# Masked attention and soft mixture of experts in one kernel: maxima and sums of the first two pairs of heads without DMA

## The chip, the cores and the metric

The kernel runs on one core of a Trainium2 chip. The metric is device time in microseconds of one execution; the runs are given by their median.

## The reference

Eight batches of eight heads with 576 positions and 64 channels: attention with a causal mask and a bias that is a difference of running sums, then a soft mixture of eight experts over all 4608 rows.

```python
scores = scale * np.matmul(q, k.transpose(0, 1, 3, 2))
s_pos = np.maximum(s, 0.0)
cum = np.cumsum(s_pos, axis=-1)
bias = -(cum[:, :, :, None] - cum[:, :, None, :])
scores = np.where(causal, -1000000000.0, scores + np.minimum(bias, 0.0))
scores = scores - np.max(scores, axis=-1, keepdims=True)
attn = np.exp(scores)
attn = attn / (np.sum(attn, axis=-1, keepdims=True) + 1e-09)
attn_out = np.matmul(attn, v)
...
logits = x @ phi
slot_input = softmax(logits, 0).T @ x
slot_out[e] = np.maximum(slot_input[e] @ w1[e], 0.0) @ w2[e]
out = softmax(logits, 1) @ slot_out
```

All is fp32. The kernel multiplies with one pass in the rounded type fp32r where it carries a number as a high and a low part.

## The kernel before, in words

The heads go in 32 pairs; head 0 of a pair lies on partitions 0 to 63 and head 1 on 64 to 127, so two products run on the two row halves of TensorE. For pair p the steps are:

- `load` fetches q and k (576 KB) into one of two raw buffers. `cast` (L341, ACT) rounds q and k to fp32r, `low` (L347, DVE) keeps the rest. A raw buffer is free when both `low` of its pair are done.
- `cum` (L357, L360) brings the running sums of the pair's heads, as a high and a low row each, to the rows of the tile `g` on its right side (`KO`). The sums of all heads are scanned once at the start on DVE (L267 to L272, tile `cum`, heads on partitions 0 to 63), split into `cumhl`, and for pairs from 4 on fetched from a copy in DRAM (`cw`, L875).
- `mx` (L378), in four groups, gives the scores with the sums in PSUM: one product with w (q and k, rounded), one with `ones2` and `g`. `red` (L389, L392, DVE) takes from it the maximum for every query, with the mask. A group takes two PSUM banks; `mx`, the scores and the small products share six banks in turn.
- `f0` (L403, L404, POOL) splits the maxima, `f1` (L411) turns them on TensorE, `f2` (L417, ACT) copies them to `hl`, and `md` (L424, L427) moves `hl` by DMA into rows of `g`, left side. Every row of `g` is then an addend of the scores.
- `s` (L445), in four groups, gives the scores in four products: high by high, k low by q high, k high by q low, and `g` by `g`, which adds the sums and takes the maxima off. `ex` (L456, ACT) takes the exponential, `cut` (L463, POOL) masks the diagonal blocks, `zc` and `z` (L477, L484 to L490) add for the sums, `a` and `ax` (L533, L522) multiply with v into y and x, `sm` (L562) adds up the sums, `ev` and `evx` copy out.
- Every fourth pair, `rw`, `rd`, `nr`, `nat`, `lt`, `c0` to `t8` normalise, turn and reduce a batch for the mixture. After the last pair the experts' weights, which come in through `pre` and `get` (L860), go through two layers, and the output is written.

Nothing schedules this at run time. The list `ORDER` (from L24) names the steps in the order in which they are recorded; each engine's queue, and SP's queue of DMA issues, holds its steps in that order and runs them so. `busy.n` in the list (L937) is n fp32 products of the identity that nobody reads.

```python
        op(("load", p), load, [dep("low", g, 0), dep("low", g, 1), ("cum", 1) if p == 2 else None])
            op(("s", p, i), (sc, i), [("md", p), ("cum", p), ("low", p, 0), ("low", p, 1)])
```

## Time and profile before

| what | us |
|---|---|
| median of 3 runs | 415.88 (414.98 to 417.01) |
| the profiled execution | 415.59 |
| its span in the trace | 413.9 |
| TensorE busy (PE) | 395.3, 96% |
| DVE busy | 284.0, 69% |
| POOL busy | 274.8, 66% |
| ACT busy | 239.6, 58% |

The profiled execution is 415.59 us, of which the trace shows a span of 413.9. A row of the page's part 5 gives an engine's line, the tile written and the tile read, shapes, count, busy time, the mean of one, and how long the engine had stood idle before them. PE is TensorE, SPq the queue of DMA issues.

### The profile page before, as it was taken

The page shows a single profiled execution, that of the slowest core. Times are in us where ns is not written, and L with a number is a line of the kernel's source. Part 1 is how long each engine was busy: PE and PEld are TensorE (multiplying, and loading weights), DVE is VectorE, ACT ScalarE, POOL GpSimd, SP SyncE. Part 2 cuts the span into 40 slices and gives each one's busy share as a digit, 9 for nine tenths or more (in the row PEclk, how much of TensorE's full clock was granted, in tenths as well). Part 3 has the DMA queues.
Part 4 walks back from the last instruction along what each step waited for, and adds up shares of the span by engine and source line. Part 5 has one row for each costly group of instructions (what it writes and reads, how often), then busy time and mean ns, then how long its engine had stood idle before and what let it go on. Part 6 is the DMA issues. An engine that isn't in the chain of part 4 may idle for free.

```text
span 413.9 us, 14533 instructions
## 1 busy us (share of the span) xinstructions
PE 395.3 (96%) x5699; PEld 295.3 (71%) x5699; DVE 284.0 (69%) x952; ACT 239.6 (58%) x717; POOL 274.8 (66%) x376
## 2 busy tenths in 40 slices
PE   8999999999999999999999999999999999999950
PEld 8778777777787777777777787778777777435540
DVE  8956887877877787778767877787778547212460
ACT  3156766586768665866586768666865663220350
POOL 7069899888878888888788878887888740000000
PEclk9999999999999999999999999999999999999995
DMA  3424578526754475447644754463236789999998
GB/s 130 133 80 140 181 260 261 171 89 202 231 172 144 146 232 172 141 148 216 188 142 144 229 176 144 146 193 110 92 89 191 250 234 401 390 412 384 306 329 295
DMA packets 35252, 83.76 MB, mean 202 GB/s; under 512 B 4976, under 2 KB 14192, under 8 KB 35184
## 3 DMA queue, kind: packets, MB, share of 16 engines
q1 hardware_dynamic: 35168, 82.83, 60.6%
q8 instruction: 45, 0.74, 0.7%
q14 instruction: 23, 0.19, 0.1%
...
HBM read 72.43 MB, written 10.03 MB: 199 GB/s over the span
## 4 chain that ended last, share of the span: by engine, by line
PE 81%; DMA 4%; DVE 3%; ACT 2%; issue 2%; SPq 0%; DVEq 0%
PE s L445 25%; PE y L533 19%; PE mx L378 11%; PE sum L562 4%; PE m L1023 3%; PE m L995 3%; DMA g<-hl 3%; PE nat L601 3%; PE lt L666 2%; PE sl L786 2%; PE mt L411 1%; PE po L1061 1%; ACT arena L456 1%; PE x L522 1%; DVE arena L392 1%
## 5 line engine op out<-in xcount | busy, mean ns | idle before, releaser
L456 ACT ACTIVATE arena<-s 128x288 f32<-128x288 f32 (+4 forms) x384 | 114.9, 407 | 31.7 <-PE s L445 30.6
L445 PE MATMUL s<-w 64*128 64x288 f32 (+4 forms) x1152 | 109.2, 304 | 0.3 <-DVE nmin L743 0.2
L533 PE MATMUL y<-arena 128*64 128x512 f32 (+4 forms) x640 | 90.8, 427 | 0.0
L445 PEld LDWEIGHTS s<-w 64*128 64x128 f32 (+1 forms) x1152 | 81.9, 177 | 10.2 <-ACT arena L456 1.2
L463 POOL TENSOR_SCALAR_AFFINE_SELECT arena<-arena 128x256 f32<-128x256 f32 (+1 forms) x160 | 63.7, 411 | 23.6 <-ACT arena L456 22.0
L484 POOL TENSOR_TENSOR arena<-arena 128x896 f32<-128x896 f32 x31 | 69.3, 2237 | 8.7 <-PE mt L411 5.9
L533 PEld LDWEIGHTS y<-arena 128*64 128x64 f32 x640 | 42.5, 137 | 44.8 <-issue 34.1
L392 DVE CUSTOM_DVE_ANT_0 arena<-mx,arena 128x448 bf16<-128x448 f32 (+3 forms) x128 | 59.0, 461 | 17.6 <-PE mx L378 15.8
L378 PE MATMUL mx<-w 64*128 64x288 f32 (+4 forms) x384 | 56.6, 302 | 0.9 <-ACT w L341 0.9
L445 PE MATMUL s<-g 64*128 64x288 f32 (+4 forms) x384 | 56.5, 291 | 0.5 <-DMA g<-hl 0.5
L392 DVE CUSTOM_DVE_ANT_0 junk<-mx,arena 64x64 bf16<-64x64 f32 (+3 forms) x128 | 49.2, 385 | 10.4 <-PE mx L378 8.7
L378 PE MATMUL mx<-g,ones 64*128 64x288 f32 (+4 forms) x384 | 53.1, 300 | 0.0
L347 DVE TENSOR_TENSOR w<-arena,w 128x576 fp32r<-128x576 f32 x64 | 50.6, 810 | 0.2
L486 POOL TENSOR_TENSOR arena<-arena 128x640 f32<-128x640 f32 x31 | 48.3, 1557 | 2.4
L341 ACT CAST w<-arena 128x576 fp32r<-128x576 f32 x64 | 40.4, 677 | 13.7 <-DMA arena<-in_qk_dram 12.7
L545 ACT COPY arena<-y 128x512 f32<-128x512 f32 x32 | 18.8, 589 | 48.8 <-PE y L533 48.8
L389 DVE TENSOR_REDUCE mx<-mx 128x1 f32<-128x288 f32 x64 | 26.7, 447 | 27.5 <-PE mx L378 23.3
L378 PEld LDWEIGHTS mx<-w 64*128 64x128 f32 x384 | 38.5, 185 | 3.2 <-ACT w L341 1.0
L378 PEld LDWEIGHTS mx<-g,ones 64*128 64x128 f32 x384 | 38.2, 185 | 0.3
L445 PEld LDWEIGHTS s<-g 64*128 64x128 f32 (+1 forms) x384 | 35.1, 177 | 1.5 <-DMA g<-hl 1.0
L488 POOL TENSOR_TENSOR arena<-arena 128x384 f32<-128x384 f32 x31 | 31.8, 1026 | 2.4
L403 POOL TENSOR_SCALAR mh<-mx 128x10 fp32r<-128x10 f32 x32 | 20.1, 627 | 17.5 <-DVE mx L392 17.1
...
## 6 DMA issues: line engine op xcount, KB each, us to landing
...
```

The costliest lines, as they stand in the source:

```text
L341: nc.scalar.copy(w[:, o:o + S], st["raw", p][:, i, :])
L347: nc.vector.tensor_tensor(w[:, o + 2 * S:o + 3 * S], st["raw", p][:, i, :], w[:, o:o + S].bitcast(F32), op=ALU.subtract)
L378: nc.tensor.matmul(ps[a][:, d:d + hi - lo], l[r], t[r, k + lo:k + hi], start=t is w, stop=t is gt)
L389: nc.vector.tensor_reduce(m[:, a, c:c + 1], ps[:, d:d + w], axis=AX.X, op=ALU.max)
L392: nc.vector.tensor_tensor_reduce(out=junk()[r, 0:w], in0=ps[r, d:d + w], in1=mask[r, o:o + w], scale=1.0, scalar=m[:, a, 4:5] if i == 1 el ...
L445: nc.tensor.matmul(ps[a][0:n, d:d + hi - lo], t[r, ko + 128 * j:ko + 128 * j + n], t[r, qo + lo:qo + hi], start=x == 0, stop=x == 3)
L456: nc.scalar.activation(st["p", p][0:n, a, o + lo:o + hi], ps[0:n, d:d + hi - lo], AF.Exp, bias=0.0, scale=0.125)
L463: nc.gpsimd.affine_select(d, d, pattern=[[0, 2], [1, n]], compare_op=ALU.is_ge, fill=0.0, base=0, channel_multiplier=-1)
L484: eng.tensor_tensor(z[:, :, 128:576], pt[:, :, 128:576], pt[:, :, 576:1024], op=ALU.add)
L486: eng.tensor_tensor(z[:, :, 256:576], z[:, :, 256:576], pt[:, :, 1024:1344], op=ALU.add)
L488: eng.tensor_tensor(z[:, :, 384:576], z[:, :, 384:576], pt[:, :, 1344:1536], op=ALU.add)
L533: nc.tensor.matmul(y[r, lo - 64:512], vt[:, j, r], st["p", p][:, g, OFF[j] + lo - 128 * j:OFF[j] + 576 - 128 * j], start=(j == 0), stop=(j ...
```

## The change

For pairs 0 and 1 the sums and maxima no longer travel by DMA:

- The sums of the 64 heads are scanned on 128 partitions: head 0 of all pairs on partitions 0 to 31, head 1 on 64 to 95, in the regions of a `u` buffer. Two memsets on DVE clear the rows between, and s comes in two DMAs, one on ACT's queue.
- `mx` of pairs 0 and 1 multiplies `cum` itself, in fp32, by a column of the identity that is broadcast to 128; it needs no `cum` step. The scores still use `g`, whose sums come from `cumhl`; the split is now `ch.0` on ACT and `ch.1` on POOL.
- `low` of pairs 0 and 1 is on POOL instead of DVE.
- `f0` of pairs 0 and 1 is on DVE and writes the split maxima into a spread operand `turn`; `f1` is 20 fp32 products of 128x32 by 128 columns that put them on the rows of `g` where they belong, into two banks; `f2` and `md` copy the banks into `g` on ACT.
- The list of steps is another one up to about pair 8; the first filler is 12 products instead of 28, and three later fillers (9, 3 and 6) are gone.

The list's beginning, before and after (its other lines read alike):

```diff
-load.0 load.1 cast.0.1 cast.0.0 cast.1.1 low.0.1 cum.0 cast.1.0 low.0.0 cum.1 low.1.1 low.1.0 load.3 busy.28 mx.0.0
+load.0 load.1 cast.0.1 cast.0.0 ch.0 busy.12 mx.0.0 cast.1.1 mx.0.1 cast.1.0 red.0.0.0 red.0.0.1 mx.0.2 red.0.1.1
...
```

The code:

```diff
@@ -232,10 +232,14 @@
         return psm.tile([128, 512], F32, tag="bank", name=name)
 
 
-    s_sb = reg("x", 0)[0:NH, 0:S]
-    ones_s = reg("x", 0)[0:NH, S:2 * S]
-    cum = reg("x", 0)[0:NH, 2 * S:3 * S]
-    nc.sync.dma_start(out=s_sb, in_=s)
+    hb = ar["u", NP % NU]
+    s_sb = arena[:, hb:hb + S]
+    ones_s = arena[:, hb + S:hb + 2 * S]
+    cum = arena[:, hb + 2 * S:hb + 3 * S]
+    nc.vector.memset(s_sb[NP:64], 0.0)
+    nc.vector.memset(s_sb[64 + NP:128], 0.0)
+    nc.sync.dma_start(out=s_sb[0:NP], in_=s[0:NP])
+    nc.scalar.dma_start(out=s_sb[64:64 + NP], in_=s[NP:NH])
     nc.gpsimd.memset(ones_s, 1.0)
 
     QO, KO = PAD, PAD + S
@@ -267,20 +271,21 @@
     nc.vector.tensor_scalar(s_sb, s_sb, 0.0, 8.0, op0=ALU.max, op1=ALU.mult)
     nc.vector.tensor_tensor_scan(out=cum, data0=ones_s, data1=s_sb, initial=0.0,
                                  op0=ALU.mult, op1=ALU.add)
-    cumhl = reg("x", 0)[0:NH, 0:2 * S].rearrange("p (l x) -> p l x", l=2)
-    nc.vector.tensor_copy(cumhl[:, 0, :].bitcast(F32R), cum)
-    nc.vector.tensor_tensor(cumhl[:, 1, :].bitcast(F32R), cum, cumhl[:, 0, :], op=ALU.subtract)
-    cumd = pd.tile([NH, 2, S], F32, tag="cum", name="cumd", bufs=1)
+    cumhl = arena[:, hb:hb + 2 * S].rearrange("p (l x) -> p l x", l=2)
+    cumd = pd.tile([2, NP, 2, S], F32, tag="cum", name="cumd", bufs=1)
 
 
     for t in gs:
         nc.gpsimd.tensor_copy(t[:, 0:KO], ones2[:, 0:1].bitcast(F32).broadcast_to([128, KO]))
     SQ = S // 8
     onesl = one.tile([128, 4 * HP + 31], F32, name="onesl")
+    dn = one.tile([128, 2, 128], F32, name="dn")
+    x0 = ar["x", 0] + 2 * DM
+    turn = arena[:, x0:x0 + 128 * NCH].rearrange("p (c k j) -> p c k j", c=NCH, j=32)
+    nc.gpsimd.memset(turn, 0.0)
+    nc.gpsimd.memset(turn[:, :, :, 0], 1.0)
     nc.gpsimd.memset(onesl, 0.0)
     nc.gpsimd.memset(onesl[:, 4 * HP - 1:4 * HP], 1.0)
-
-    dn = one.tile([128, 2, 128], F32, name="dn")
     nc.gpsimd.memset(dn[64:128, 1, :], 0.0)
     nc.gpsimd.memset(reg("x", 0)[64:128, 0:DM], 0.0)
     for i in range(NPB):
@@ -314,6 +319,9 @@
 
     def every32(t, i):
         return t.bitcast(F32).rearrange("(a r) x -> a r x", r=32)[:, i, :]
+
+    op(("ch", 0), lambda: nc.scalar.copy(cumhl[:, 0, :].bitcast(F32R), cum))
+    op(("ch", 1), lambda: nc.gpsimd.tensor_tensor(cumhl[:, 1, :].bitcast(F32R), cum, cumhl[:, 0, :], op=ALU.subtract), [("ch", 0)])
 
     def scores(p):
 
@@ -344,7 +352,7 @@
             use("raw", p, NR)
             use("w", p, NW)
             o = (WQ, WK)[i]
-            nc.vector.tensor_tensor(w[:, o + 2 * S:o + 3 * S], st["raw", p][:, i, :],
+            (nc.gpsimd if p < 2 else nc.vector).tensor_tensor(w[:, o + 2 * S:o + 3 * S], st["raw", p][:, i, :],
                                     w[:, o:o + S].bitcast(F32), op=ALU.subtract)
         g = old(NW)
         war = [("s", g, i) for i in range(4)] if g is not None else []
@@ -352,16 +360,16 @@
             op(("cast", p, i), (cast, i), [("load", p)] + war)
             op(("low", p, i), (low, i), [("cast", p, i)])
 
-        def cum():
+        def cums():
             if p >= HP:
-                nc.sync.dma_start(out=every32(gt, 0)[:, KO:KO + S], in_=cumd[2 * p:2 * p + 2])
+                nc.sync.dma_start(out=every32(gt, 0)[:, KO:KO + S], in_=cumd[:, p])
                 return
             for a in range(2):
-                (nc.scalar if a and p == 0 else nc.sync).dma_start(out=every32(gt, 0)[2 * a:2 * a + 2, KO:KO + S],
-                                                                   in_=cumhl[2 * p + a:2 * p + a + 1, :, :])
+                nc.sync.dma_start(out=every32(gt, 0)[2 * a:2 * a + 2, KO:KO + S],
+                                  in_=cumhl[64 * a + p:64 * a + p + 1, :, :])
         g = old(NG)
         war = [("s", g, i) for i in range(4)] if g is not None else []
-        op(("cum", p), cum, war + [("cw",)] * (p >= HP))
+        op(("cum", p), cums, war + [("cw",) if p >= HP else ("ch", 1)])
 
 
         groups = [[(0, 4, 0, 288)], [(0, 4, 288, 576)], [(0, 3, 0, 448), (448, 0, 0, 64)],
@@ -373,10 +381,11 @@
             st["m", p, i] = ps
             for (d, c, lo, hi) in groups[i]:
                 q0 = WQ + sum(QC[c])
-                for l, t, k in ((w[:, q0 - 128:q0], w, WK), (ones2, gt, KO)):
+                for l, t, k in ((w[:, q0 - 128:q0], w, WK), (ones2, gt, KO) if p > 1 else (None, cum, 0)):
                     for a, r in enumerate(half):
-                        nc.tensor.matmul(ps[a][:, d:d + hi - lo], l[r], t[r, k + lo:k + hi],
-                                         start=t is w, stop=t is gt)
+                        x = ident[r, 64 * a + p:64 * a + p + 1].broadcast_to([64, 128]) if l is None else l[r]
+                        nc.tensor.matmul(ps[a][:, d:d + hi - lo], x, t[r, k + lo:k + hi],
+                                         start=t is w, stop=t is not w)
 
         def red(i, a):
             if i == 0 and a == 0:
@@ -393,12 +402,17 @@
                     out=junk()[r, 0:w], in0=ps[r, d:d + w], in1=mask[r, o:o + w], scale=1.0,
                     scalar=m[:, a, 4:5] if i == 1 else NEG, op0=ALU.add, op1=ALU.max, accum_out=m[r, a, c:c + 1])
         for i in range(4):
-            op(("mx", p, i), (mxp, i), [("cast", p, 0), ("cast", p, 1), ("cum", p), dep("f0", old(3))])
+            op(("mx", p, i), (mxp, i), [("cast", p, 0), ("cast", p, 1), ("cum", p) if p > 1 else None, dep("f0", old(3))])
             for a in range(2):
                 op(("red", p, i, a), (red, i, a), [("mx", p, i), ("red", p, 0, a) if i else None])
 
         def f0():
             use("mx", p, 3)
+            if p < 2:
+                mh = [turn.rearrange("p c (a l) j -> p a l c j", a=2)[:, :, l, :, 1] for l in range(2)]
+                nc.vector.tensor_scalar(mh[0].bitcast(F32R), m, 1.0, None, op0=ALU.mult)
+                nc.vector.tensor_tensor(mh[1].bitcast(F32R), m, mh[0], op=ALU.subtract)
+                return
             mh = p2.tile([128, 2, 2, NCH], F32R, tag="mh", name=f"mh{p}")
             nc.gpsimd.tensor_scalar(mh[:, :, 0, :], m, 1.0, None, op0=ALU.mult)
             nc.gpsimd.tensor_tensor(mh[:, :, 1, :], m, mh[:, :, 0, :].bitcast(F32), op=ALU.subtract)
@@ -406,6 +420,13 @@
         op(("f0", p), f0, [("red", p, i, a) for i in range(4) for a in range(2)] + [dep("f1", old(2))])
 
         def f1():
+            if p < 2:
+                st["mt", p] = [bank(f"mt{i}") for i in range(2)]
+                for c in range(NCH):
+                    for k in range(4):
+                        nc.tensor.matmul(st["mt", p][c // 4][32 * k:32 * k + 32, 128 * (c % 4):128 * (c % 4) + 128],
+                                         turn[:, c, k, :], ident, start=True, stop=True)
+                return
             mh = st.pop(("mh", p))
             ps = bank("mt")
             nc.tensor.transpose(ps[0:4 * NCH, 0:128], mh.rearrange("p a l c -> p (a l c)").bitcast(F32), ident)
@@ -413,19 +434,19 @@
         op(("f1", p), f1, [("f0", p), dep("md", old(2))])
 
         def f2():
+            if p < 2:
+                nc.scalar.copy(gt[:, 0:512], st["mt", p][0])
+                return
             hl = p2.tile([4 * NCH, 128], F32R, tag="hl", name=f"hl{p}", bufs=1)
             nc.scalar.copy(hl, st.pop(("mt", p))[0:4 * NCH, 0:128])
             st["hl", p] = hl
         op(("f2", p), f2, [("f1", p)])
 
         def md():
-            hl = st.pop(("hl", p))
-            if p:
-                nc.sync.dma_start(out=every32(gt, 1)[:, 0:KO].rearrange("l (c q) -> l c q", c=NCH), in_=hl.bitcast(F32))
+            if p < 2:
+                nc.scalar.copy(gt[:, 512:KO], st["mt", p][1][:, 0:KO - 512])
                 return
-            for a in range(2):
-                (nc.scalar if a and p == 0 else nc.sync).dma_start(out=every32(gt, 1)[2 * a:2 * a + 2, 0:KO].rearrange("l (c q) -> l c q", c=NCH),
-                                  in_=hl[2 * NCH * a:2 * NCH * (a + 1)].bitcast(F32))
+            nc.sync.dma_start(out=every32(gt, 1)[:, 0:KO].rearrange("l (c q) -> l c q", c=NCH), in_=st.pop(("hl", p)).bitcast(F32))
         op(("md", p), md, [("f2", p)])
 
 
@@ -872,7 +893,10 @@
     op(("sit", 0), sit0, [prev, ("t8", B - 1)])
     op(("sit", 1), sit1, [("sit", 0)])
     op(("cst",), (fetch, g4, cst[:, 0:128]), [("load", 3)])
-    op(("cw",), lambda: nc.sync.dma_start(out=cumd, in_=cumhl), [("cum", 1)])
+    def copy_cum():
+        for a in range(2):
+            nc.sync.dma_start(out=cumd[a], in_=cumhl[64 * a:64 * a + NP])
+    op(("cw",), copy_cum, [("cum", 1)])
     op(("phi",), load_phi, [("load", 2)])
     ops["lt", 0][1].append(("phi",))
 
@@ -1158,7 +1182,7 @@
     HP = H // 2
 
     phi = moe_phi.reshape(HP, 128, -1).transpose(1, 0, 2)
-    arrays = dict(qk=qk, v=vn, s=s.reshape(B * H, S), phi=phi, w1=w1, w2=w2, cst=constants())
+    arrays = dict(qk=qk, v=vn, s=s.reshape(B * H // 2, 2, S).transpose(1, 0, 2).reshape(B * H, S), phi=phi, w1=w1, w2=w2, cst=constants())
     return {n: np.ascontiguousarray(a) for n, a in arrays.items()}
```

What the change makes of two queues, as the built programs list them. First TensorE, from the last maxima of pair 1 that come ahead of the first scores (`s_0`); `mx_1` are maxima of pair 1, `w_101` and `w_104` its rounded q and k, `mt` the banks of the turn. Before:

```order
L378 MATMUL mx_1_0_296<-w_101 128x448
L378 MATMUL mx_1_1_297<-w_101 128x448
L378 MATMUL mx_1_0_296<-g_98,ones_109 128x448
L378 MATMUL mx_1_1_297<-g_98,ones_109 128x448
L378 MATMUL mx_1_0_296<-w_101 128x64
L378 MATMUL mx_1_1_297<-w_101 128x64
L378 MATMUL mx_1_0_296<-g_98,ones_109 128x64
L378 MATMUL mx_1_1_297<-g_98,ones_109 128x64
L937 MATMUL busy<-ident 128x128 x6
L445 MATMUL s_0_0_323<-w_100 128x288
```

Now:

```order
L387 MATMUL mx_1_0_217<-arena,ident 128x64
L387 MATMUL mx_1_1_218<-arena,ident 128x64
L427 MATMUL mt_236<-ident,arena 32x128 x16
L427 MATMUL mt_237<-ident,arena 32x128 x4
L387 MATMUL mx_1_0_269<-w_104 128x288
L387 MATMUL mx_1_1_270<-w_104 128x288
L387 MATMUL mx_1_0_269<-arena,ident 128x288
L387 MATMUL mx_1_1_270<-arena,ident 128x288
L466 MATMUL s_0_0_277<-w_103 128x288
```

The filler ahead of the first scores is gone, the 20 products of the turn stand two groups of products before them, and the last group of pair 1's maxima (320 and 192 columns) has moved behind the first scores.

Then POOL, from its last memsets to the first masks (`L463`, now `L484`); `mh` are the split maxima. Before:

```order
L285 MEMSET arena 64x512
L287 MEMSET arena 64x2x64 x2
L288 MEMSET acc 128x512
L403 TENSOR_SCALAR mh_257<-mx_115 128x2x5
L404 TENSOR_TENSOR mh_257<-mx_115,mh_257 128x2x5
L403 TENSOR_SCALAR mh_354<-mx_117 128x2x5
L404 TENSOR_TENSOR mh_354<-mx_117,mh_354 128x2x5
L463 AFFINE_SELECT arena<-arena 128x2x128 x3
```

Now:

```order
L290 MEMSET arena 64x512
L292 MEMSET arena 64x2x64 x2
L293 MEMSET acc 128x512
L324 TENSOR_TENSOR arena<-arena 128x576
L355 TENSOR_TENSOR w_103<-arena,w_103 128x576 x2
L355 TENSOR_TENSOR w_104<-arena,w_104 128x576 x2
L484 AFFINE_SELECT arena<-arena 128x2x128 x3
```

Four tiny instructions on the maxima have left POOL's queue, and five subtractions of 576 columns have come in ahead of the first mask.

## Rows read from the trace of the kernel before

**Rows 1.** The page: busy time of the engines, and the chain's shares by line.

```profile
PE 395.3 (96%) x5699; PEld 295.3 (71%) x5699; DVE 284.0 (69%) x952; ACT 239.6 (58%) x717; POOL 274.8 (66%) x376
...
PE s L445 25%; PE y L533 19%; PE mx L378 11%; PE sum L562 4%; PE m L1023 3%; PE m L995 3%; DMA g<-hl 3%; PE nat L601 3%; PE lt L666 2%; PE sl L786 2%; PE mt L411 1%; PE po L1061 1%; ACT arena L456 1%; PE x L522 1%; DVE arena L392 1%
```

**Rows 2.** TensorE's waits, whole span: us in total, times, longest us.

```profile
PE busy L937 <- POOL ident masks.py:199: 1.4, 1, 1.4
PE mx L378 <- ACT w L341: 0.9, 1, 0.9
```

**Rows 3.** The chain that ended last, 0 to 60 us: start us, us, what.

```profile
18.67 1.08 PE mx L378 x11
19.76 1.53 PE busy L937 x12
21.29 3.41 PE s L445 x48
...
25.33 0.21 PE mt L411
25.54 1.01 PE y L533 x4
...
29.64 2.81 PE s L445 x40
```

**Rows 4.** Stretch 350 to 380: busy of five engines, granted clock, DMA share, GB/s.

```profile
350.00:380.00 30.00, 29.80 (x342) 14.72 (x340) 7.78 (x22) 5.93 (x14) 0.45 (x1) 1.00 1.02 403
```

**Rows 5.** Timeline of the start, four engines: start us, us, instruction, count.

```profile
1.07 1.15 DVE L251 MEMSET g<- 128x576 f32 x2
...
4.50 1.67 DVE L268 TENSOR_TENSOR_SCAN arena<-arena 64x576 f32<-64x576 f32 x1
5.38 1.25 ACT L341 CAST w<-arena 128x576 fp32r<-128x576 f32 x2 [3.31 <-DMA arena<-in_qk_dram]
...
8.31 0.53 POOL L288 MEMSET acc<- 128x512 f32 x1
...
10.71 0.34 SPq L331 DMA_DIRECT2D arena<-in_qk_dram  x1
...
11.25 0.82 DVE L389 TENSOR_REDUCE mx<-mx 128x1 f32<-128x288 f32 x2 [0.56 <-PE mx L378]
...
15.17 0.62 DVE L392 CUSTOM_DVE_ANT_0 arena<-mx,arena 128x448 bf16<-128x448 f32 x1
...
16.09 0.82 DVE L389 TENSOR_REDUCE mx<-mx 128x1 f32<-128x288 f32 x2
...
17.22 0.67 ACT L341 CAST w<-arena 128x576 fp32r<-128x576 f32 x1 [7.32 <-DMA arena<-in_qk_dram]
...
22.50 2.81 ACT L456 ACTIVATE arena<-s 128x288 f32<-128x288 f32 x10 [3.88 <-PE s L445]
```

**Rows 6.** One line of POOL: shortest, median and longest ns, first and last start.

```profile
L277 POOL CAST g<-ones x3: 717/944/1771, 3.4 to 4.9; 128x640 fp32r<-128x640 f32 x3
```

**Rows 7.** The chain near 346 us: products of 128 columns, 32 rows of output each.

```profile
346.31 0.22 PE lt L666 x8
```

**Rows 8.** Line L937 in two stretches of the start: ns, first and last start.

```profile
L937 PE MATMUL busy<-ident x7: 421/421/421, 5.2 to 6.5; 128*128 128x128 f32 x7
L937 PE MATMUL busy<-ident x11: 274/275/275, 7.3 to 8.4; 128*128 128x128 f32 x11
```

**Rows 9.** Groups by form: count, busy us, mean ns, idle before.

```profile
L486 POOL TENSOR_TENSOR arena<-arena 128x640 f32<-128x640 f32 x31 | 48.3, 1557 | 2.4
L488 POOL TENSOR_TENSOR arena<-arena 128x384 f32<-128x384 f32 x31 | 31.8, 1026 | 2.4
L545 ACT COPY arena<-y 128x512 f32<-128x512 f32 x32 | 18.8, 589 | 48.8 <-PE y L533 48.8
```

**Rows 10.** Two stretches in which TensorE did nothing; the granted clock is third from the end.

```profile
18.00:18.60 0.60, 0.00 (x0) 0.00 (x0) 0.60 (x5) 0.60 (x2) 0.00 (x0) 1.00 0.00 0
404.00:406.00 2.00, 0.00 (x0) 0.00 (x0) 0.00 (x0) 0.00 (x0) 0.00 (x0) 0.50 1.01 345
```

More of the change, by code (lines that the diff above doesn't have):

```diff
@@ new lines @@
+low.29.0 f0.28 t4.5 s.27.2 ex.27.0.0 low.29.1 ex.27.0.1 s.27.1 load.31 ex.27.2.0 cut.27.0 mx.29.0 ex.27.2.1 sm.26
+ex.27.1.0 red.29.0.0 cut.27.2 red.29.0.1 ex.27.1.1 f1.28 t5.5 f2.28 cut.27.1 zc.27 s.27.3 md.28 t6.5 z.27.0 mx.29.3
+ex.27.3.0 cum.30 mx.29.2 ex.27.3.1 red.29.3.0 cast.30.1 mx.29.1 red.29.3.1 cast.30.0 a.26.0 cut.27.3 red.29.2.0 z.27.1
+a.26.1 red.29.2.1 a.26.2 a.26.3 z.27.2 red.29.1.0 a.26.4 ax.27 ev.26 load_v.28 red.29.1.1 s.28.0 low.30.0 evx.27
+z.27.3 s.28.2 low.30.1 ex.28.0.0 f0.29 ex.28.0.1 s.28.1 ex.28.2.0 get.0 cut.28.0 mx.30.0 ex.28.2.1 sm.27 ex.28.1.0
@@ L164 @@
+c0.7 t2.7 t3.7 busy.1 m.0 nat.31 t8.6 nat.28 m.1 nat.29 natd.31 natd.28 m.2 natd.29 nat.30 m.3 t4.7 nat0.7 m.4 natd.30
+c1.7 get.21 natd0.7 t5.7 m.5 get.22 t6.7 busy.2 m.6 t7.7 m.7 s0.7 s1.7 ct t8.7 get.26 get.19 get.17 get.10 sit.0
+get.24 get.25 get.23 sit.1 s2.7 s2p.7
 """
```

266 lines of the change are left out of this document (129 added, 137 removed).

## The prediction

> **What bounds the kernel now.** I read the page first: TensorE is busy for 395.3 of 413.9 us [rows 1]. The list of TensorE's waits then says how little of the rest is idling: the longest entries are 1.4 us for the identity at the start and 0.9 us for a cast [rows 2]. So the time is TensorE's queue, and an edit pays only by taking work off that queue or by filling it earlier. The chain of the first 60 us shows where it is filled with nothing: behind the first maxima stand filler products (L937), the first scores (L445) begin at 21.29 us, the second pair's at 29.64 [rows 3]. After 21.29 I see no wait of TensorE in that chain. What lies ahead of 21.29 is a latency chain over DVE, DMA and ACT, and the change works on that chain. From the maxima of pair 8 on, TensorE's order is the same in both programs, and the other engines' from about pair 9, so a lead that is there at pair 8 should reach the end.
>
> The tail must move too. From 350 to 380 us the DMA engines are at 1.02 of their share while TensorE works 29.80 of 30 us [rows 4]; those weight loads go into buffers that the last pairs free, so they are released earlier by the same amount.
>
> **The chain to the first scores, step by step.** Times are from the span's start.
>
> 1. *Sums.* The scan ends at 6.2 (4.50 + 1.67) [rows 5]. Two memsets of 576 columns now come ahead of it on DVE; two such took 1.15 [rows 5]. That gives cum at 7.3. The scan can also meet one of three like casts on POOL, of which the quickest took 717 ns and the slowest 1771 [rows 6]; against this stands that DVE waited a little for s there, which the memsets use up. I let the two cancel and keep 0.7, a whole cast, for the range. The Trainium skill (SBUF — State Buffer, "SBUF: two separate sides") says that a GpSimd instruction and a DVE one with two SBUF inputs shut each other out for their whole length; the 1771 agrees, and by that rule the sum would have cum at up to 8.0.
>
> 2. *First product.* It needs the casts of q and k (5.38 + 1.25 = 6.6) and now cum itself instead of two DMA landings. The fp32 products with cum are new; their nearest row is L533, fp32 on two column halves at once, 1.01 us for 512 columns [rows 3]. So 288 columns cost 0.57 and the first reduction can start at 7.9, where it started at 11.25. If the two row halves did not overlap, each price would double; I take the row's and keep the double for the range.
>
> 3. *Maxima of pair 0.* DVE ran them without a gap from 11.25 to 16.09, so 4.84 us [rows 5]. TensorE's share for a pair is about 0.7 for the half with w (L378 has 11% of the span for 32 pairs, 1.4 with both halves [rows 1]) plus 3.2 for 1600 columns with cum, 3.9 in all, less than DVE's 4.84; the third group, 0.25 + 1.01, comes some 0.3 after DVE is ready for it. End at 13.05. The split into high and low moves from POOL to DVE, two tiny instructions: 0.4, between nothing and the 0.8 of two reductions. 13.45.
>
> 4. *Turn.* Twenty fp32 products of 128x32 with 128 columns, 40 passes. The row of that shape is L666, 8 in 0.22 us [rows 7]: 1.1 us. One by one they would take 4.4, at the later pace of the filler (11 starts from 7.3 to 8.4, 0.11 each [rows 8]). L666 has the same four column groups, so I take 1.1: 14.55. Two ACT copies follow; the first (0.59 by L545 [rows 9]) can start when 16 of the 20 are done, the second has a quarter of its columns, 0.3. The row is in place at about 15.2. The DMA to the left side, behind which filler stood in the queue, is gone.
>
> 5. *Bank.* The first scores need PSUM banks that DVE frees only after four reductions of pair 1: 0.82 for the two short ones and 0.92 for each pair of 448 and 64 columns (15.17 to 16.09) [rows 5], 2.6 in all, from 13.45 to 16.05. This is later than 15.2, so it decides: **first scores at 16.05, 5.2 us earlier than 21.29.**
>
> 6. *POOL* now subtracts for cum and for both operands of pairs 0 and 1, five instructions of 576 columns. Between 1026 ns (384) and 1557 (640) [rows 9] that is 1.42, with gaps 1.5. Its memsets ended at 8.84 (8.31 + 0.53) [rows 5]; they start about 1.1 later behind DVE's memsets and get 0.8 more for the spread operand (640 columns, by the 0.53 of 512, and a short one), so 10.8; then 12.3 for cum, 15.3 for both operands of pair 0, 18.3 for pair 1. The scores use pair 0's low parts in their second and third product, so 15.3 is hidden by 16.05 with 0.7 to spare. DVE's 3 us for them leave its queue.
>
> **What is given back.** At 21.29 the old queue had done all maxima of pairs 0 and 1 and the first group of pair 2. At 16.05 the new one still owes the last group of pair 1 (512 columns: 0.25 + 1.0 = 1.25) and the first of pair 2 (0.4 of the 1.08 us in [rows 3]); and pair 1's turn costs 1.1 where L411 took 0.21: 0.9 more. That is 2.55. Filler is not counted: it fills waits.
>
> **New waits** between first and second scores: pair 1's maxima end behind its last fp32 group, about 0.3 us after TensorE is ready to turn them. The load of pair 2 has to wait for POOL's subtracts of pair 0 (two raw buffers), 15.3 instead of 10.71, and behind it in SP's queue stand v of pair 0, the load of pair 3 and cum of pair 2. Load 2 was issued at 10.71 and its cast ran at 17.22 with another load in flight; the first load, alone at the start, was cast at 5.38 [rows 5]. So load 2 lands some 4 to 5 us after 15.3, at 19 to 20. ACT comes to its cast at about 18.8 (16.05, 1.0 for 480 of the 1600 columns of the scores' 3.41, and 1.7 for six exponentials at 2.81 for ten [rows 3, 5]), and ACT's queue is in order: behind the cast stand exponentials that free banks and the copies of pair 1's turn. I put nothing for this in the sum and 1 us in a rival.
>
> **Sum.** 5.24 - 2.55 - 0.3 = 2.4 us. The profiled execution took 415.59 us (span 413.9), 0.29 under the median of 415.88. So 413.2 against the profiled one, and **413.5 against the median, 0.6% less**. About 0.5% (2.1 us) is what a measurement of this kernel can tell from no change.
>
> **The rivals.**
>
> *POOL and the loads keep back half.* At 1.9 each (the casts went up to 1771 [rows 6]), POOL's five end at 20.3 instead of 18.3: pair 0's low parts come at 16.5, the scores 0.5 late, and with loads 2 and 3 going out later ACT waits about 1 us for a cast. Gain 2.4 - 0.5 - 1 = 0.9: 415.0. For it: the whole chain of loads now hangs on POOL. Against it: DVE's reductions read PSUM and only a mask from SBUF, and the mean of L486 beside them is 1557 for the larger shape. 0.15.
>
> *The clock (slower).* The first filler products took 421 ns each, 275 from 7.3 us on [rows 8]: TensorE began at 1.2 GHz and rose to 2.4 while it worked without a pause. The granted clock reads 1.00 in the pause at 18.0 and 0.50 from 404 us on, after TensorE's last work [rows 10]. The change cuts the filler at the start from 28 to 12 products, 24 passes, which at the slow pace (7 starts from 5.2 to 6.5 [rows 8]) last to about 6.5; the queue then pauses for cum, near where the clock rose. If it stays at 1.2 GHz, the 7.6 us that TensorE does before the first scores (3.9 + 0.7 + 1.25 + 1.1 + 0.7) take 15.2: first scores near 22 with the same 2.55 owed, so 3.3 us *slower*: 419.2. It decides from where the low clock lasts to about 14.6 us: lost is half of the time after 7.3, less the 1.2 by which DVE is the slower in step 3. The Trainium skill (TensorE: Matmul & The Clock Gate, Part 1) says that the low clock is the default and activity releases it; the 421 and 275 agree. Against the rival: the queue is filled for most of 7.3 to 16. 0.12 for slower; 0.05 for a rise between, which eats the gain (415.9).
>
> *The end does not move.* If the saturated DMA of the tail held the end by itself, 2.4 us at the front would give nothing: 415.9. Against it: TensorE has no wait for a weight among its longest [rows 2], and the loads hang on buffers it frees. 0.04.
>
> **How the numbers follow.** The forecast has 0.64 and its own range from 411.7 to 414.4: the upper gain of 4.2 has the first scores at 15.2 (step 5's bank free in time) and only 1.9 owed (the last group of pair 1 at 0.6, as a group with `ones2`); the lower, 1.5, has an ACT wait of 0.9. I put 0.52 of the 0.64 past 2.1 us and 0.12 below. Faster 0.52; same 0.12 + 0.15 + 0.05 + 0.04 = 0.36; slower 0.12. The range of 8 in 10 goes from 411.2 to 416.0: it takes in the cases without gain and leaves out the low clock and a little below. Cum products at the double price (6.4 + 0.7 for pair 0, 2.3 over DVE's 4.84) and cum at 8.0 lie inside it too.
>
> **What would show it.** First product with cum near 7.4 and first reduction near 7.9; 40 passes of the turn in about 1.1 us; first scores at 16.0, the second pair's near 24.3 with 2.5 us of maxima and y still owed; POOL's last subtract near 18.3. Wrong would be: first maxima at twice their price past 9 us; an ACT wait of over 1 us for a load; scores before 15 or after 17.5; or pair 8 reached less than 1 us earlier although pair 1 was 2.4 earlier.

## The result

The changed kernel took 419.55 us (median of 5 runs, 418.92 to 420.93), the kernel before beside it 416.43 (414.98 to 417.16): ratio 1.0093, 95% interval 1.0069 to 1.0118. It is **slower by 3.1 us**; 413.5 had been predicted, with 416.0 as the upper end. The profiled execution after took 418.92 us (span 417.2).

TensorE's list of waits (us in total, times, longest us) names the places:

```profile
PE lt L687 <- DVE mx L401: 1.7, 1, 1.7
PE nat L622 <- DVE mx L401: 1.0, 1, 1.0
PE mt L427 <- DVE arena L414: 0.9, 1, 0.9
PE s L466 <- DVE mx L401: 0.5, 1, 0.5
```

Beside these there is again the identity's 1.4. Before, the longest after it was 0.9 for a cast [rows 2]; behind each of these four stands DVE. DVE's busy time doesn't show it: 285.3 us now, 284.0 then [rows 1].

**The start** came nearly as forecast. Its timeline (start us, us, engine, line, operation, count; in brackets the idle time before, and what ended it):

```profile
7.89 0.82 DVE L398 TENSOR_REDUCE mx<-mx 128x1 f32<-128x288 f32 x2 [0.84 <-PE mx L387]
12.13 5.51 POOL L355 TENSOR_TENSOR w<-arena,w 128x576 fp32r<-128x576 f32 x4
13.60 1.32 DVE L414 TENSOR_TENSOR arena<-mx,arena 128x10 fp32r<-128x10 f32 x1
14.97 1.29 PE L427 MATMUL mt<-ident,arena 128*32 128x128 f32 x38 [0.88 <-DVE arena L414]
16.70 0.78 PE L466 MATMUL s<-w 64*128 64x288 f32 x6
19.71 1.29 ACT L349 CAST w<-arena 128x576 fp32r<-128x576 f32 x2
```

The first scores start at 16.70, 4.6 us earlier than 21.29 [rows 3]. One row is odd: L414, DVE's subtraction of ten columns that makes the low half of the split, takes 1.32 us beside POOL's subtractions L355. Pair 1's, with POOL idle, takes 0.18.

**Then the lead goes in three steps.** The stretches, from the timelines of POOL, DVE and TensorE:

```profile
51.81 2.08 POOL L505 TENSOR_TENSOR arena<-arena 128x896 f32<-128x896 f32 x1
52.06 2.45 DVE L355 TENSOR_TENSOR w<-arena,w 128x576 fp32r<-128x576 f32 x1
57.97 0.85 PE L466 MATMUL s<-w 64*128 64x448 f32 x5 [0.50 <-DVE mx L401]
...
80.61 2.12 POOL L505 TENSOR_TENSOR arena<-arena 128x896 f32<-128x896 f32 x1
82.12 1.58 DVE L614 TENSOR_TENSOR arena<-arena 128x576 f32<-128x576 f32 x1 [1.36 <-DMA arena<-rs]
84.44 0.43 PE L687 MATMUL lt<-arena 128*32 128x128 f32 x8 [1.67 <-DVE mx L401]
...
278.12 2.12 POOL L505 TENSOR_TENSOR arena<-arena 128x896 f32<-128x896 f32 x1
278.26 2.60 DVE L614 TENSOR_TENSOR arena<-arena 128x576 f32<-128x576 f32 x1
281.60 0.66 PE L622 MATMUL nat<-ident,arena 128*128 128x128 f32 x4 [1.05 <-DVE mx L401]
```

Each time a DVE instruction with both operands in SBUF (`low`, L355; `nr`, L614) runs beside POOL's sums `z` (L505), and takes 1.6 to 2.6 us where 0.75 is usual. Below, such an overlap is called a **meeting**, and the instruction that it stretches is **shut out**. Behind it in DVE's queue stand the reductions of the maxima, and TensorE waits for the PSUM banks that they free. Two stretches (busy of five engines, granted clock, DMA share, GB/s) show that TensorE stands still for half of a microsecond at the first loss, and that behind the second it works at 0.50, its lower level of 1.2 GHz (the granted clock reads 0.76 from 85 to 86 and 0.53 from 88 to 89):

```profile
57.00:58.00 1.00, 0.50 (x9) 0.25 (x6) 0.94 (x5) 0.71 (x3) 0.09 (x1) 1.00 0.33 133
...
86.00:88.00 2.00, 2.00 (x21) 1.72 (x13) 1.94 (x9) 0.91 (x2) 0.28 (x2) 0.50 1.05 391
```

The kernel before has the same pair of instructions at the second place, and there it costs DVE nothing:

```profile
80.97 0.75 DVE L593 TENSOR_TENSOR arena<-arena 128x576 f32<-128x576 f32 x1
81.00 2.70 POOL L484 TENSOR_TENSOR arena<-arena 128x896 f32<-128x896 f32 x1
...
90.61 0.28 PE L411 MATMUL mt<-ident,mh 128*20 128x128 f32 x1
...
379.94 0.70 PE L1035 MATMUL sel<-pre 128*128 128x256 f32 x2 [0.18 <-DVE pre L1030]
```

DVE was first by 0.03 us; it is POOL's row that is longer, 2.70 for 2.12. The last two rows are marks of TensorE's progress, the turn of pair 8 and the selection near the end. In the kernel after they are:

```profile
93.05 0.28 PE L432 MATMUL mt<-ident,mh 128*20 128x128 f32 x1
...
382.98 0.70 PE L1059 MATMUL sel<-pre 128*128 128x256 f32 x2 [0.17 <-DVE pre L1054]
```

So TensorE is 2.4 us late at pair 8 and 3.0 at the end. The expectations below call this a **lag**: TensorE's matmuls are counted by columns through all its rows, and the lag at a moment of the kernel before is how much later (+) or earlier (-) the other kernel has as many still to issue. Up to pair 8, where the orders differ, the lag depends on how columns are counted, by about half a microsecond; from 91 us on it doesn't. The times are medians, the lags are from the profiled executions; e1 to e12 are the experiments that follow:

| kernel | us (ratio to before, interval) | 47 | 59 | 79 | 91 | 259 | 399 |
|---|---|---|---|---|---|---|---|
| after | 419.55 (1.0093, 1.0069 to 1.0118) | -1.1 | +0.6 | -0.6 | +2.4 | +1.9 | +3.0 |
| e1 | 414.18 (0.9961, 0.9938 to 0.9984) | -1.1 | -1.1 | -0.8 | -0.8 | -1.9 | -1.9 |
| e2 | 420.33 (1.0122, 1.0092 to 1.0152) | +1.5 | +3.4 | +2.2 | +5.4 | +4.4 | +4.4 |
| e3 | 416.15 (1.0013, 0.9987 to 1.0038) | -1.6 | +0.1 | -1.1 | +0.9 | -0.3 | -0.3 |
| e4 | 418.18 (one run) | -1.2 | +0.5 | -0.7 | +1.3 | +1.3 | +2.4 |
| e5 | 418.60 (1.0065, 1.0041 to 1.0088) | -1.1 | +0.6 | -0.6 | +2.7 | +1.8 | +2.8 |
| e6 | 416.27 (1.0006, 0.9988 to 1.0025) | -1.1 | -1.0 | -2.3 | -0.3 | -0.7 | +0.3 |
| e9 | 417.44 (1.0043, 1.0017 to 1.0070) | +0.2 | +1.9 | +0.7 | +2.9 | +2.3 | +3.4 |
| e8 | 413.54 (0.9938, 0.9917 to 0.9959) | -2.0 | -2.0 | -2.0 | -2.0 | -3.0 | -3.1 |
| e10 | 415.59 (0.9987, 0.9967 to 1.0007) | -1.1 | +0.7 | -0.6 | -0.3 | 0.0 | 0.0 |
| e12 | 417.03 (1.0029, 1.0002 to 1.0056) | -1.1 | +0.7 | -0.6 | +0.9 | +1.0 | +1.0 |
| e11 | 412.92 (0.9938, 0.9915 to 0.9960) | -1.3 | -1.2 | -2.4 | -2.0 | -3.0 | -3.0 |

The lag of one profiled execution and the medians can differ by a microsecond. e9, whose edit lies at 80 us, has 1.3 more already at 47, because TensorE's clock fell at its start: the turn takes 2.36 us there for the 1.29 above, and the first scores start at 18.21 instead of 16.70 (e9, a row and a stretch):

```profile
14.97 2.36 PE L427 MATMUL mt<-ident,arena 128*32 128x128 f32 x38 [0.89 <-DVE arena L414]
...
15.00:17.00 2.00, 2.00 (x38) 1.73 (x38) 1.91 (x7) 0.00 (x0) 2.00 (x2) 0.50 0.53 124
```

Between 155 and 203 us the profiled execution of the kernel before loses some 1.0 that e8 and e11 don't lose; their leads grow by that.

### The profile page after: what moved, and what is told of

The parts are those of the page before. It is cut to its first block, busy times and chain, and to the rows that moved or that the text cites. A ratio compares the mean times of both kernels' runs of the same rounds, so it can differ in the third digit from the quotient of the medians.

```text
span 417.2 us, 14600 instructions
## 1 busy us (share of the span) xinstructions
PE 395.7 (95%) x5733; PEld 293.5 (70%) x5733; DVE 285.3 (68%) x952; ACT 241.5 (58%) x720; POOL 281.8 (68%) x379
## 4 chain that ended last, share of the span: by engine, by line
PE 80%; DVE 7%; DMA 4%; issue 2%; ACT 1%; POOL 1%; SPq 1%; DVEq 0%
PE s L466 24%; PE y L554 18%; PE mx L387 11%; PE sum L583 4%; PE m L1047 3%; PE m L1019 3%; PE nat L622 3%; DMA arena<-rs 2%; PE lt L687 2%; PE sl L807 2%; DMA g<-hl 2%; PE mt L432 1%; PE po L1085 1%; DVE arena L401 1%; DVE arena L614 1%
## 5 line engine op out<-in xcount | busy, mean ns | idle before, releaser
L484 POOL TENSOR_SCALAR_AFFINE_SELECT arena<-arena 128x256 f32<-128x256 f32 (+1 forms) x160 | 65.5, 424 | 27.8 <-ACT arena L477 26.1
L505 POOL TENSOR_TENSOR arena<-arena 128x896 f32<-128x896 f32 x31 | 68.3, 2205 | 7.8 <-PE mt L432 5.5
L401 DVE CUSTOM_DVE_ANT_0 arena<-mx,arena 128x320 bf16<-128x320 f32 (+3 forms) x128 | 59.4, 464 | 14.8 <-PE mx L387 13.2
L387 PE MATMUL mx<-w 64*128 64x288 f32 (+4 forms) x384 | 59.1, 313 | 0.1
L466 PE MATMUL s<-g 64*128 64x288 f32 (+4 forms) x384 | 57.5, 292 | 0.1
L401 DVE CUSTOM_DVE_ANT_0 junk<-mx,arena 128x192 bf16<-128x192 f32 (+3 forms) x128 | 48.7, 381 | 9.4 <-PE mx L387 7.6
L355 DVE TENSOR_TENSOR w<-arena,w 128x576 fp32r<-128x576 f32 x60 | 49.1, 834 | 0.9 <-POOL mh L418 0.8
L387 PE MATMUL mx<-g,ones 64*128 64x288 f32 (+1 forms) x360 | 48.7, 299 | 0.0
L387 PEld LDWEIGHTS mx<-g,ones 64*128 64x128 f32 x360 | 34.7, 186 | 0.4
L614 DVE TENSOR_TENSOR arena<-arena 128x576 f32<-128x576 f32 x30 | 26.1, 885 | 1.8 <-DMA arena<-rs 1.8
```

Source lines behind the costliest of these rows:

```text
L355: (nc.gpsimd if p < 2 else nc.vector).tensor_tensor(w[:, o + 2 * S:o + 3 * S], st["raw", p][:, i, :], w[:, o:o + S].bitcast(F32), op=ALU.s ...
L387: nc.tensor.matmul(ps[a][:, d:d + hi - lo], x, t[r, k + lo:k + hi], start=t is w, stop=t is not w)
L401: nc.vector.tensor_tensor_reduce(out=junk()[r, 0:w], in0=ps[r, d:d + w], in1=mask[r, o:o + w], scale=1.0, scalar=m[:, a, 4:5] if i == 1 el ...
L466: nc.tensor.matmul(ps[a][0:n, d:d + hi - lo], t[r, ko + 128 * j:ko + 128 * j + n], t[r, qo + lo:qo + hi], start=x == 0, stop=x == 3)
L484: nc.gpsimd.affine_select(d, d, pattern=[[0, 2], [1, n]], compare_op=ALU.is_ge, fill=0.0, base=0, channel_multiplier=-1)
L505: eng.tensor_tensor(z[:, :, 128:576], pt[:, :, 128:576], pt[:, :, 576:1024], op=ALU.add)
```

## Start and order apart

**e1** keeps the change's code and its order up to the scores of pair 1, and puts the steps behind them in the order of the kernel before. **e2** is the kernel before, with its own first 84 steps and the change's order behind them. Both edit the list alone:

```diff
-ORDER = changed order
+ORDER = changed order, up to s.1.0 + old order, what is left      (e1)
-ORDER = old order
+ORDER = old order, first 84 steps + changed order, what is left   (e2)
```

> The changed kernel, but from the second pair's first scores on the steps stand in the order of the kernel before. Theory A (the new order of pairs 2 to 8 lost the time, the new start gained): the changed kernel had a lead of 1.4 us over the one before from 27 to 55 us of the span, so this one ends 1.0 to 1.8 us below the kernel before, about 415. Theory B (the new start itself costs it, by what it moves on POOL and in the loads): the loss comes back under the old order too, 418.5 to 419.5.

> The kernel before, but from the second pair's v on the steps stand in the changed kernel's order (pairs 1 to 8). Theory A: from a lead of 1.4 to a lag of 2.4 the new order lost 3.8 us, so this one is 2.5 to 4.5 us slower than the kernel before, about 420. Theory B: within 1 us of the kernel before.

Theory A holds on both sides. With the old order behind the new start the lead stays and the kernel is 0.4% faster than before (2.1 us, a little more than expected); with the new order behind the old start it is 1.2% slower. In e2 the wait before `lt` is there without any change at the start, and so are the two rows behind it:

```profile
83.36 2.12 POOL L484 TENSOR_TENSOR arena<-arena 128x896 f32<-128x896 f32 x1
...
83.54 2.92 DVE L593 TENSOR_TENSOR arena<-arena 128x576 f32<-128x576 f32 x1
```

## The split

**e3** puts POOL's first subtraction for pair 0 behind the split, by a tiny copy on POOL that reads what the split's first instruction writes. **e4** leaves POOL as it is and makes the split's second instruction one with a single SBUF operand; it multiplies by zero, so the low parts of the maxima of pairs 0 and 1 are left out.

```diff
+if p == 0 and i == 0:                                              # e3, in low
+    gate = one.tile([128, 2], F32, name="gate")
+    nc.gpsimd.tensor_copy(gate, turn[:, 0, 0, 1:3])
...
-nc.vector.tensor_tensor(mh[1].bitcast(F32R), m, mh[0], op=ALU.subtract)       # e4, in f0
+nc.vector.tensor_scalar(mh[1].bitcast(F32R), m, 0.0, None, op0=ALU.mult)
```

(In e3 `low.0.1` also goes ahead of `low.0.0` in the list, and the gated `low.0.0` behind `f0.0`.)

> The changed kernel; POOL's second subtraction for pair 0 (q) waits for DVE's split of pair 0's maxima (a tiny POOL copy reads its output first). Theory A1 (DVE's subtraction of two SBUF operands, 1.32 us, was shut out by POOL's subtraction): it takes 0.2 to 0.4 us, the first scores begin 0.8 to 1.1 us earlier, near 15.7. Theory A2 (it is slow by itself, for its spread output): 1.3 us again, first scores not before 16.5. The whole time: 0 to 1 us less than the changed kernel if the rest of the order does not give it back.

> The changed kernel; DVE's second instruction of the split of the maxima of pairs 0 and 1 has one SBUF operand (it multiplies by zero), so the low parts of these maxima are left out. A1: 0.2 to 0.5 us instead of 1.32, although POOL's subtractions run beside it as before. A2: 1.3 us again.

The timeline of e3, and of e4:

```profile
13.61 0.18 DVE L417 TENSOR_TENSOR arena<-mx,arena 128x10 fp32r<-128x10 f32 x1
13.64 0.20 POOL L357 COPY gate<-arena 128x2 f32<-128x2 f32 x1
```

```profile
12.14 5.56 POOL L355 TENSOR_TENSOR w<-arena,w 128x576 fp32r<-128x576 f32 x4
13.49 0.16 DVE L414 TENSOR_SCALAR arena<-mx 128x10 fp32r<-128x10 f32 x1
```

A1 holds, by e3: out of POOL's way the same subtraction takes 0.18. e4 shows less than it was made for. Its instruction starts at 13.49, 0.01 us ahead of the second of POOL's four subtractions (13.50), so it came first, and the run can't tell one operand from two. One SBUF operand alone is no protection: the split's first instruction, L413, has one and takes 0.37 in e4 beside POOL's first subtraction and 0.18 for pair 1, and in all kernels a small one, L741 in after, takes 0.65 beside a sum of POOL and 0.17 otherwise (e4, then after):

```profile
13.21 0.37 DVE L413 TENSOR_SCALAR arena<-mx 128x10 fp32r<-128x10 f32 x1
...
333.78 1.56 POOL L507 TENSOR_TENSOR arena<-arena 128x640 f32<-128x640 f32 x1
334.72 0.65 DVE L741 TENSOR_SCALAR cs<-cs 128x5 f32<-128x5 f32 x1
```

DVE's reductions, which read PSUM and a mask, are not stretched: 448 columns take 0.62 us beside POOL's sums and away from them. The first scores start at 15.58 and 15.46 instead of 16.70. The first loss (2.43 us for `low.6.0`) is in e3 as before. The second is there too, but the granted clock stays at 1.00 behind it, and the lag grows by 2.0 between 79 and 91 where it grew by 3.0. The third is gone, as the two instructions now meet in the other order there. So e3 is 3.4 us below the changed kernel where 0 to 1 had been expected, and most of that comes from places at which the edit doesn't aim.

## The first loss

**e6** moves one step, `low.6.0`, behind the reductions of pair 5:

```diff
-... red.5.3.0 mx.5.2 cut.3.3 zc.3 cum.6 low.6.0 a.3.0 z.3.0 ... red.5.2.1 s.4.0 ... low.6.1
+... red.5.3.0 mx.5.2 cut.3.3 zc.3 cum.6 a.3.0 z.3.0 ... red.5.2.1 low.6.0 s.4.0 ... low.6.1
```

> The changed kernel, with one subtraction of DVE (low.6.0, L355, 2.45 us at 52.06 beside POOL's sums L505 at 51.81) put behind the reductions of pair 5, ahead of low.6.1. Theory C1: the first loss is this one instruction, shut out by POOL's sums; then it takes 0.75 to 1.0 at about 56, the reductions of pair 5 end some 2 us earlier, the half-clock slice 57 to 58 is gone, and the lag against the kernel before at 60 us is about -1.5 instead of +0.3; if the later places are unchanged the time is 417.2 to 418.2. Rival C2: the subtraction meets the next sums (L507) and is shut out as long, or the reductions wait for something else there, and the lag at 60 stays between -0.3 and +0.5. Either way the lead may be lost again at 82 to 88 us: then the lag at 87 is near 2 and the time about 419.

C1 holds. Both subtractions of pair 6 now run one behind the other in 1.43 us, and the turn of pair 5 starts at 57.39:

```profile
55.48 1.43 DVE L355 TENSOR_TENSOR w<-arena,w 128x576 fp32r<-128x576 f32 x2
...
57.39 0.28 PE L432 MATMUL mt<-ident,mh 128*20 128x128 f32 x1
...
79.30 2.72 DVE L614 TENSOR_TENSOR arena<-arena 128x576 f32<-128x576 f32 x1 [0.23 <-DMA arena<-rs]
```

In the changed kernel the same turn is 1.67 us later:

```profile
59.06 0.28 PE L432 MATMUL mt<-ident,mh 128*20 128x128 f32 x1
```

That is the first loss. TensorE's list shows only 0.5 of it as a wait; in the rest its products ahead of the turn take longer (1.12 for 0.71 us in one group of six). The lag at 59 is -1.0. (The “half-clock slice” of the expectation was a misreading: the 0.50 of that row is TensorE's busy time, its clock there was 1.00.) The time came out lower than expected, 416.27 for 417.2 to 418.2: the second loss is there (the row at 79.30: `nr.3`, now shut out for 2 us), but without the stretch of half clock.

## The second loss: transfer, queue or meeting

`nr.3` at 82.12 had waited 1.36 us for the broadcast of the reciprocal sums, which took 6.93 us with weight loads on its heels. Three theories stood against each other. **e5** takes the weight loads away from it, **e9** puts the waiting instruction behind the first four of the reductions that it held up (two steps):

```diff
-... s.6.0 pre.3 red.7.1.0 pre.1 ... red.8.0.0 pre.5 ... nr.3 pre.4 ... lt.3 pre.6
+... s.6.0 red.7.1.0 ... red.8.0.0 ... nr.3 ... lt.3 pre.3 pre.1 pre.5 pre.4 pre.6    (e5)
...
-... natd.2 nr.3 pre.4 ... red.8.3.1 cast.9.0
+... natd.2 pre.4 ... red.8.3.1 nr.3 cast.9.0                                         (e9)
```

> The changed kernel, with the four weight loads pre.3, pre.1, pre.5 and pre.4 taken from SP's order around the broadcasts of rd.2 and rd.3 (from 75.74 us on) and put behind lt.3, past the place where nr.3 waits. Theory B1: the second loss is DMA crowding, the broadcast of rd.3 is late because weight loads were issued on its heels; then it lands by about 79 instead of 82.1, DVE's idle 1.36 before nr.3 (L614) at 82.1 is gone, TensorE's pause of 1.67 before lt at 84.4 shrinks below 0.7, the stretch at half clock from 85.8 to 88.6 is gone, and the lag against the kernel before at 87 us falls from 2.4 to 0.5 or less; the time about 416.5 to 417.5. Rival B2: nr.3, once its data is there, meets POOL's sums z.5.0 (L505, 80.6 to 82.7) and is shut out by them until 82.7, so the lag at 87 falls by less than 0.7 and the time is 418.5 or more. Rival B3: something else, the lag unchanged.

> The changed kernel, with the multiplication nr.3 (L614, which waits for the broadcast rd.3 until 82.1) put four reductions later in DVE's order, behind red.8.3.1. Theory B1 together with DVE's order (the reductions stand queued behind a wait for a transfer): the reductions of pair 8 run at about 81 to 83, TensorE's lt has its banks by about 82.6, the pause of 1.67 and the half-clock stretch are gone, the lag at 87 us is 0 to 0.7 and the time 416.5 to 417.5, though the transfer is as late as it was (6.9 us). Rival B2/B3, the transfer's lateness has no part in it: the lag stays above 1.7 and the time above 418.5.

B1 falls. In e5 the data is there in time, and DVE starts 0.08 us behind POOL:

```profile
80.60 2.12 POOL L505 TENSOR_TENSOR arena<-arena 128x896 f32<-128x896 f32 x1
...
80.68 3.01 DVE L614 TENSOR_TENSOR arena<-arena 128x576 f32<-128x576 f32 x1
```

TensorE's pause before `lt` is 1.7 us again and the lag at 91 is 2.7. In e9 the moved `nr.3` meets the next sum, behind it by 0.01 us, and `lt` now waits for `nr.3` itself, since it reads its product:

```profile
84.45 1.54 POOL L507 TENSOR_TENSOR arena<-arena 128x640 f32<-128x640 f32 x1
...
84.46 2.14 DVE L614 TENSOR_TENSOR arena<-arena 128x576 f32<-128x576 f32 x1
```

That is B2, the meeting, though in the changed kernel itself the late transfer covered most of it. The lateness is not steady either: with the loads in the same order `nr.3` waits 0.57 us for the broadcast in e3, 0.23 in e6 and not at all in e4, and is shut out in all three. e9's time speaks less plainly. Its 417.44 lies in the range that B1 gave, 2.1 us below the changed kernel, while its lag at 91, 2.9 with 1.3 from its start, lies nearer to the rival's; the execution that was profiled, 419.01, is the second slowest of twelve. So it is e5 and e10 that decide for B2, and e9 shows only that the moved instruction meets the next sum. **e10** is e5 with the order of the meeting turned round at the second and the third place; **e12** has the same two copies without e5's move of the loads:

```diff
 def zs(i):
+    if i == 0 and p in (6, 25):
+        nc.gpsimd.tensor_copy(one.tile([128, 2], F32, name=f"gate{p}"), st["u", {6: 3, 25: 21}[p]][:, 0:2])
     if i == 0: eng.tensor_tensor(z[:, :, 128:576], ...)
```

> The kernel of e5 (the changed one, four weight loads later), and two tiny copies on POOL that read the products of nr.3 and nr.21 (L614), put ahead of the sums z.6.0 and z.25.0 (L505; what the expectation of e5 called z.5.0 is z.6.0): so POOL's sums start behind DVE's multiplication instead of 0.07 and 0.14 us ahead of it. Theory B2 with its third place: the second and the third loss are nr.3 (3.01 at 80.7) and nr.21 (2.60 at 278.1) shut out by those sums, so with DVE first each takes 0.75, the lag against the kernel before is between -0.5 and +0.7 at 87 us where it was 2.6, TensorE's pauses of 1.7 before lt and 1.1 before nat are gone, no stretch at half clock is left at 86, and the lag makes no step of 1.1 at 279; the end is 2.5 to 3.5 us below that of e5, 415.2 to 416.2. Rival: the sums that are now late hold the cuts or the sums matrix products behind them, or the transfer is what counts after all, and the time stays above 417.3.

> The changed kernel with the two tiny copies of e10 on POOL, the sums z.6.0 and z.25.0 behind nr.3 and nr.21, but the weight loads where the change has them, so the broadcast of rd.3 is late. If both the late transfer and the shut-out have to go for the second loss (each one covers the other): nr.3 starts at 82.1 as in the changed kernel and takes 0.75, TensorE's pause before lt is 0.7 to 1.1 where it was 1.7, the lag against the kernel before is 1.2 to 2.2 at 87 us and makes no step at 279, and the time is 417.0 to 418.0. If the shut-out alone made the loss, the lag at 87 is below 0.5 and the time that of e10, 415.6.

In e10 (DVE, then POOL):

```profile
80.68 0.75 DVE L616 TENSOR_TENSOR arena<-arena 128x576 f32<-128x576 f32 x1
...
81.49 0.19 POOL L505 COPY gate<-arena 128x2 f32<-128x2 f32 x1 [0.82 <-DVE arena L616]
81.63 2.12 POOL L507 TENSOR_TENSOR arena<-arena 128x896 f32<-128x896 f32 x1
```

Same start of `nr.3` to the hundredth as in e5, 0.75 for 3.01, and 3.0 us off the time (415.59 for 418.60; the third place is won as well, and about as much is lost at another, told at the end). POOL waits 0.82 for this, and it costs nothing that the time shows. There is no step at 279.

e12 came out within its range of time, but not by the way that it names. In this execution the broadcast came at 80.9 and `nr.3` took 0.76; the crowding fell on the next transfer in the queue instead, the row of maxima for pair 7's scores, for which TensorE then waited 1.5 us (chain of e12: start us, us, what):

```profile
81.31 6.85 DMA g<-hl
```

So the weight loads cost about 1.4 us once the shut-out is gone (417.03 for 415.59, from two sets of runs); they fell on one transfer in the changed kernel's profiled execution and on another in e12's. Taken away alone they gave 0.95 (418.60 for 419.55), with intervals that overlap: in e5 the shut-out holds `nr.3` until 83.69, and in the changed kernel it ended at 83.70.

## Putting it together

**e8** is e1 with e3's edit. **e11** is the changed kernel in its own order, with the edits of e3, e6 and e10 (in which e5's is): all four meetings apart, nothing else.

> The first experiment's kernel (the change's start, the order of the kernel before from the scores of pair 1 on) with the third one's edit as well: POOL's first subtraction stands behind a tiny copy that reads the turned maxima, so it can't run beside the split. If the two effects add: the first scores at 15.6 instead of 16.7, a lead against the kernel before of 1.5 to 2.5 from 31 us on where it was 1.0, and the time 412.8 to 413.8, 0.6 to 0.8% below the kernel before. Rival: the lead of 1.1 is taken back before pair 8 by a wait that the order of the kernel before has anyway (a lead of 0.8 to 1.0 at 80 us), and the time stays at 414 to 414.5.

> The changed kernel in its own order with all four meetings of a DVE instruction with a POOL instruction taken apart: POOL's first subtraction behind the split (as in e3), low.6.0 behind the reductions of pair 5 (as in e6), the weight loads later (e5) and z.6.0 and z.25.0 behind nr.3 and nr.21 (e10). If the whole loss is these four, the lead that the prediction had at pair 1 goes through to the end: a lag against the kernel before of -2.5 to -1.5 from 31 to 80 us, -2.5 to -1.0 from 87 us to the end, and a time of 413.4 to 415.0, faster than before by 0.3 to 0.7%. Rival: the new order has losses of its own besides (banks, casts, transfers), some of the lead goes in another place, and the time is 415.5 or more.

```profile
88.63 0.28 PE L435 MATMUL mt<-ident,mh 128*20 128x128 f32 x1
...
376.96 0.70 PE L1064 MATMUL sel<-pre 128*128 128x256 f32 x2 [0.18 <-DVE pre L1059]
```

Both are faster than the kernel before by 0.6%; their intervals overlap almost wholly, so neither is the better. e11 is a little below its range of time. Its lead at 47 and 59 is smaller than the expected 1.5 to 2.5, though: taking the split's meeting apart brings the first scores 1.1 us forward, but at 47 us it is worth 0.9 in the old order (e8 against e1) and 0.2 to 0.5 in the new one (e11 and e3). The four meetings and the loads that stood on one of them account for the change's whole loss: 419.55 with them, 412.92 without, and the marks of e11 are 2.0 and 3.0 us ahead of the kernel before where after was 2.4 and 3.0 behind. The old order has as many such instructions on DVE, only other meetings: in e8 `nr.3` starts at 78.95 and POOL's sum at 78.97. Not every shut-out costs time. The kernel before has the one below and e1 doesn't, yet e1 gains nothing on it between 59 and 79 us:

```profile
69.63 2.12 POOL L484 TENSOR_TENSOR arena<-arena 128x896 f32<-128x896 f32 x1
...
70.36 2.00 DVE L593 TENSOR_TENSOR arena<-arena 128x576 f32<-128x576 f32 x1 [0.86 <-DMA arena<-rs]
```

## Why the prediction was wrong

**The step that failed** is the sentence that a lead at pair 8 should reach the end, because the order is the same from there on; it was used for a lead at pair 1. The change orders the steps of pairs 2 to 8 anew, and this stretch was not walked: the sum has no term for it. The first loss lies in it, 1.7 us at 52 to 59 (e6). And the same order doesn't carry a lead over either. By the two lists, DVE's steps agree from `red.8.0.0` on and POOL's from `z.5.1` on. `nr.3` and `z.6.0`, whose meeting made the second loss, stand behind those places, and so do `nr.21` and `z.25.0` of the third. The second cost 3.0 us at 82 to 89 (e10 against e5), the third 1.1 at 278. Each engine's own order was as before; which of the two came first at the meeting was not. At the third place DVE had been 0.21 us ahead of POOL in the kernel before, and after the change it was 0.14 behind:

```profile
275.96 0.75 DVE L593 TENSOR_TENSOR arena<-arena 128x576 f32<-128x576 f32 x1
...
276.17 2.53 POOL L484 TENSOR_TENSOR arena<-arena 128x896 f32<-128x896 f32 x1
```

By the prediction's steps:

1. *Sums*, and 2. *First product*: right. First reduction at 7.89, forecast 7.9; the fp32 products cost about what L533's row gave.
3. *Maxima, split*: the maxima right, the split wrong. 0.4 forecast, with 0.8 as the upper end; 1.7 from 13.21 to 14.92, because its second instruction was shut out by POOL. That is 1.1 us of the 16.70 (e3). The prediction quoted the Trainium skill (SBUF — State Buffer, "SBUF: two separate sides") on this exclusion in step 1, for a scan and a cast, and did not put the same question to an instruction it had itself moved to DVE. The same section (under “Who interferes with whom”) says that issue order, not the operation's shape, decides who blocks. The trace agrees: 0.75 and 2.70 in one order, 3.01 and 2.12 in the other, at starts 0.03 and 0.08 us apart.
4. *Turn*: nearly right. 40 passes take 1.3 to 1.4, 1.1 forecast; in the changed kernel the wait for the split stands inside it as well.
5. *Bank*: too late by half a microsecond. Without the shut-out the scores start at 15.46 to 15.58, so the bank is free by then and 16.05 was not the bound.
6. *POOL*: right. 1.38 each, the last ends at 17.64, forecast 18.3. But "DVE's reductions read PSUM" answered only for the reductions; `low` and `nr` read both operands from SBUF.

*Given back*: too small. In e8, where the old order follows, 11.97 us pass from the first scores (15.58) to the second pair's (27.55), and 8.35 before [rows 3]: 3.6 given back, 2.55 and 0.3 forecast. First scores half a microsecond earlier than forecast make up for part of it, so that the lead is 2.0 from 47 to 91 us, 2.4 forecast. That e8 then ends at 413.54, the forecast time, is partly luck: its lead at the end is 3.1 because of what the kernel before loses between 155 and 203 us, which the prediction doesn't have. *The load of pair 2*: cast at 19.71, forecast 19 to 20, and no wait of ACT shows.

**The rivals.** POOL and the loads keeping back half came nearest in its engine, but not in place or price: its low parts were in time, its sums were in DVE's way. The low clock at the start is not what happened in the changed kernel: its granted clock reads 1.00 from 7 us to the second loss, and TensorE's work at the start went at the forecast pace. It isn't refuted as a risk: in e9, whose program is the same up to 80 us, the clock rose in time too but fell to 0.50 at 15 us, behind the pause before the turn, and put the first scores off by 1.5 us. The pause is as long in the changed kernel, without the fall. The end that does not move fell too: the selection moves by the lag in after and e11 alike. The slower side of the prediction had one mechanism, at the start, and the real one began 35 us behind it. The sign to look for was named, though: "pair 8 reached less than 1 us earlier although pair 1 was 2.4 earlier".
